# Moving steps between slots in a pooled-attention and maxout kernel: an earlier first sum, a shorter warm-up, batches 1 and 2 re-slotted, a split last store

## The chip, the cores and the metric

One core of one Trainium2 chip. The metric is the device time of one execution in microseconds (us), median over executions. The span is the part of it that the trace covers, from the first to the last instruction; it is shorter than the time by 1.8 us on average in nearly all kernels here. All runs compared are in the fast state, unless a single run's state is unknown, which is said.

## The reference, cut to what matters

```python
# q, k, v: (8 batches, 8 heads, 576 rows, 64); w1, w2, w3: (512, 768); w_out: (768, 512)
k_p = k.reshape(B, H, 72, 8, D).mean(axis=3)          # pool 8 rows of k and of v
v_p = v.reshape(B, H, 72, 8, D).mean(axis=3)
attn = softmax(q @ k_p.T / sqrt(D))
x = (attn @ v_p)  -> (4608 tokens, 512)
h = max(x @ w1, x @ w2, x @ w3)
out = h @ w_out                                       # (4608, 512) float32
```

## The kernel before

TensorE (PE) is fed by one hand-ordered program. The tokens go in nine blocks of 512: for each block a *hidden* stage (three products and their maximum) and a *project* stage (four output blocks of 128 tokens, `po`). The attention of the next batch is cut into steps (`pool_k`, `turn_k`, `turn_q`, `scores`, `values`, `turn_x`) that are put between the pieces of hidden and project. A piece is called a slot. The steps wait on copies by VectorE (DVE) and ScalarE (ACT), so a step in too early a slot stalls PE.

The names that matter: `turn_k` transposes the pooled k and fills `kz` with two DVE copies, `turn_q` transposes q (`pqt` to `qT`), `scores` gives `psc`, whose exponential is `et`, `values` gives `pav` and then `rcp` and `xn` on DVE ("v0" to "v4"), `turn_x` transposes `xn` (`pxt`) and copies it to `xT` ("x0" to "x4"), which the hidden stage (`pw`) reads.

```python
    heat(16)                                  # 16 warm-up matmuls, then per third of k:
    for i in (0, 2, 4):
        c = slice(i, i + 2)
        nc.vector.tensor_tensor(out=k16[:, c], in0=kts[0][:, c, 0:4],
                                in1=kts[0][:, c, 4:8], op=ALU.add)
        for p in pkp0:
            for j in range(4):
                nc.tensor.matmul(p[:, c], identh[0:96, :], k16[:, c, j, :], ...)
        if i > 0:
            ...                               # copies of the sums to kp, on DVE and ACT
        if i < 4:
            heat(1)
# ... batch 1: its steps between the slots of block 0
    steps = {19: 1, 20: 1, 21: 1, 22: 1, 23: 1, 24: 2, 25: 2, 26: 2}
    out1 = outputs(1)                         # v0 v1 x0 v2 x1 v3 x2 v4 x3 x4, xT copies on ACT
# ... batch 2: its steps between the slots of block 1
    PLAN1 = (9, 11, 13, 15, 18, 19, 20, 21, 22, 23, 24, 25, 26, 26, 27, 27, 28, 28, 29,
             29, 30, 30)
# ... the output blocks
            po = psp.tile([128, C], F32, name="po", tag="pw", bufs=3)
            ...                               # 6 matmuls of 512 columns into po
            nc.scalar.copy(out=osb, in_=po)
            for u in range(2):
                nc.sync.dma_start(out=dst[:, GS[g], :], in_=osb[64 * u:64 * u + 64, :])
```

The softmax here doesn't subtract the row's maximum and nothing guards it: scores larger than these inputs give would overflow.

Of the kernel before, what the change touches and what calls it, by code (L numbers as in the profile page):

```python
# [10 lines left out]
ALU = mybir.AluOpType  # L11
# [3 lines left out]
def kernel(  # L15
# [11 lines left out]
    nc = tc.nc  # L27
    dt = mybir.dt
    F32, BF16, F16 = dt.float32, dt.bfloat16, dt.float16

    B, H, S, D = q.shape
    POOL = 8
    Sp = S // POOL
    C = H * D
# [7 lines left out]
    NG = 9  # L42
    GS = (0, 2, 4, 6, 8, 1, 3, 5, 7)
# [157 lines left out]
    def new_et(b):  # L201
        ets[b] = sb2.tile([Sp, H, S], F16, name="et", tag="et")
# [37 lines left out]
    def queries(b):  # L240

        new_et(b)
        for m, (n0, n1) in enumerate(((0, 5), (5, 10), (10, 14), (14, 18))):
            turn_q(b, n0, n1, nc.scalar.copy, TR)
            yield
            if m == (3 if b == 2 else 2) and b > 1:
                turn_k(b)
                yield
        for h in range(H):
            scores(b, h)  # L250
            yield

    def outputs(b, tags=(TR,) * 5):

        last = None
        for (c0, keep), tag in zip(CHUNKS, tags):
            xn = values(b, c0)
            yield
            if last:
                turn_x(*last)  # L260
                yield
            last = (b, c0, keep, xn, tag)
        turn_x(*last)
        yield

# [31 lines left out]
    def project(n, hT):  # L297
        for mm in range(4):
            m = 4 * n + mm
            po = psp.tile([128, C], F32, name="po", tag="pw", bufs=3)  # L300
            for jc in range(JCH):
                nc.tensor.matmul(po, hT[:, jc, bass.ts(mm, 128)],  # L302
                                 wo_sb[:, jc, :],
                                 start=(jc == 0), stop=(jc == JCH - 1))
            osb = sb3.tile([128, C], F32, name="osb", tag="osb", bufs=5)
            nc.scalar.copy(out=osb, in_=po)  # L306
            for u in range(2):
                b, g = divmod(2 * m + u, NG)
                dst = out[S * b:S * b + S, :].rearrange("(r g) c -> r g c", g=NG)
                nc.sync.dma_start(out=dst[:, GS[g], :], in_=osb[64 * u:64 * u + 64, :])  # L310
            yield
# [7 lines left out]
    def heat(n):  # L319
        for _ in range(n):  # L320
            nc.tensor.matmul(wm, warm[:, 0:128], warm, start=True, stop=True)  # L321
# [6 lines left out]
            for _ in range(2)]  # L328
    heat(16)
    for i in (0, 2, 4):  # L330
        c = slice(i, i + 2)
        nc.vector.tensor_tensor(out=k16[:, c], in0=kts[0][:, c, 0:4],
                                in1=kts[0][:, c, 4:8], op=ALU.add)
        for p in pkp0:
            for j in range(4):
                nc.tensor.matmul(p[:, c], identh[0:96, :], k16[:, c, j, :],  # L336
                                 start=(j == 0), stop=(j == 3))
        if i > 0:
            c = slice(i - 2 if i == 2 else i, i + 2)
            nc.vector.tensor_copy(out=kps[0][:, c, 0, :], in_=pkp0[0][0:96, c])  # L340
            nc.scalar.copy(out=kps[0][:, c, 1, :], in_=pkp0[1][0:96, c])
        if i < 4:
            heat(1)
    turn_q(0, 0, 5, nc.scalar.copy, PW)
    turn_q(0, 5, 9, nc.vector.tensor_copy, ATT)
    pkt0 = [keys(0, PW) for _ in range(2)]
    for h in (0, 4):
        fill_kz(0, 0, h, h + 4, pkt0[0], nc.vector.tensor_copy)
        fill_kz(0, 1, h, h + 4, pkt0[1], nc.scalar.copy)
    heat(1)  # L350

# [14 lines left out]
    turn_q(0, 9, 14, nc.vector.tensor_copy, PW)  # L366
    turn_q(0, 14, 18, nc.scalar.copy, PW)
    pool_v(0, 0, 4, PW, nc.vector.tensor_copy)
# [13 lines left out]

    def rest():
        for c0, keep in CHUNKS[2:]:
            xn0.append(values(0, c0))
            yield
            if c0 > 256:
                turn_x(0, last, 0, xn0[-2], TR)
                yield
            last = c0  # L390
        turn_x(0, last, keep, xn0[-1], TR)
        yield


    nc.vector.memset(kz_all[1], 0.0)
    hT0 = new_hT()
    out0 = rest()

    def early():
        pool_k(1, TR)  # L400
        yield
        turn_k(1)
        yield
        yield from queries(1)

    side = early()
    steps = {19: 1, 20: 1, 21: 1, 22: 1, 23: 1, 24: 2, 25: 2, 26: 2}
    for slot, _ in enumerate(hidden(0, hT0)):
        if slot > 0:
            next(out0, None)  # L410
        for _ in range(steps.get(slot, 0)):
            next(side)
    out1 = outputs(1)
    for mm, _ in enumerate(project(0, hT0)):
        if mm == 0:
            pool_v(1, 0, 4, TR, nc.scalar.copy)
            next(side)
            pool_v(1, 4, 8, PW, nc.vector.tensor_copy)
        next(side, None)
        if mm > 0:  # L420
            next(out1)
        if mm > 1:
            next(out1)
# [8 lines left out]
    def batch(b):  # L432
        yield from queries(b)
        yield from outputs(b)


    PLAN = (2, 4, 5, 6, 8, 8, 9, 10, 11, 12, 13, 14, 15, 16, 17, 18, 18, 19, 19, 20,
            20, 21)
    PLAN1 = (9, 11, 13, 15, 18, 19, 20, 21, 22, 23, 24, 25, 26, 26, 27, 27, 28, 28, 29,
             29, 30, 30)  # L440
    for n in range(1, TOK // NB):
# [50 lines left out]
```

## Time and profile before

| | before |
|---|---|
| time, median of 3 | 264.79 us (264.77 to 265.23) |
| profiled execution | 265.15 us, span 263.4 |
| first hidden stage starts | 18.98 us |
| PE gaps in batch 1 (30 to 57 us) | 4.0 us |
| PE gaps in batch 2 (65 to 84 us) | 1.6 us |
| last output block's first matmul to the end of the span | 6.1 us |

A gap is counted from the start of the last matmul plus its steady spacing to the start of the next; the prediction below has the spacings. Warm-up matmuls count as work in this sum although they give nothing.

The table doesn't show where the clock of the array turns from half to full speed. In the timeline of the kernel before (start, duration, engine, line, operation, tiles, count, then the idle time ahead and what ended it):

```profile
6.99 0.15 PEld L321 LDWEIGHTS <-warm 128*128 128x128 bf16 x1 [0.28 <-issue]
7.33 0.10 PEld L321 LDWEIGHTS <-warm 128*128 128x128 bf16 x1 [0.20 <-issue]
...
8.86 0.42 DVE L340 CAST kp<-pkp 96x256 bf16<-96x256 f32 x1 [1.74 <-PE pkp L336]
...
18.98 1.04 PE L272 MATMUL pw<-xT,mw 128*128 128x256 f16 x8
```

The warm-up's weight loads stand 0.43 us apart up to 6.99, then 0.34, then 0.22. The step of 0.34 is part slow and part fast, so the clock turned at about 7.25 us. DVE waited 1.74 us for the sums of k before it could copy them.

### The profile page before, as it was taken

To read this page: it belongs to the slowest core of one execution; us is meant where nothing else is said; L and a number is where in the kernel's file an instruction comes from. 1 tells how busy PE (TensorE), PEld (TensorE's weight loads), DVE (VectorE), ACT (ScalarE), POOL (GpSimd) and SP (SyncE) were. 2 spreads that over 40 slices of the span, in tenths; PEclk is the share of its full clock that TensorE was granted. 3 is DMA by queue.
4 is the path that set the end of the run, shared out by engine and by line. 5 is a ranking of instruction groups with operands and counts; after the bars stand their busy time and mean duration, and the time that the engine had idled before them with its cause. 6 is when DMAs were issued, how large, how long until landed. Compare 5 with 4: busy or idle time off the path is not lost.

```text
span 263.4 us, 4734 instructions
## 1 busy us (share of the span) xinstructions
PE 251.3 (95%) x1900; PEld 142.1 (54%) x1900; DVE 129.5 (49%) x233; ACT 131.3 (50%) x234; POOL 117.6 (45%) x84
## 2 busy tenths in 40 slices
PE   7899989889999999999999999999999999999992
PEld 2678646477455555555555555555555554444441
DVE  3567552365544546364635564455446554523440
ACT  1374247546555474647464646564656553133221
POOL 8563001999899999898980796000000000000000
PEclk9999999999999999999999999999999999999999
DMA  7999999887767977968987605100420042015006
GB/s 179 202 196 207 201 230 231 216 228 146 157 170 163 251 188 146 252 212 165 205 212 206 94 2 122 40 2 0 105 58 0 2 100 59 2 36 124 0 9 154
DMA packets 20867, 34.73 MB, mean 132 GB/s; under 512 B 2636, under 2 KB 13260, under 8 KB 20268
## 3 DMA queue, kind: packets, MB, share of 16 engines
q0 software_dynamic: 14048, 21.44, 41.7%
q1 hardware_dynamic: 6796, 12.98, 19.9%
q8 instruction: 15, 0.25, 0.4%
q14 instruction: 8, 0.07, 0.1%
HBM read 34.60 MB, written 9.44 MB: 167 GB/s over the span
## 4 chain that ended last, share of the span: by engine, by line
PE 89%; ACT 6%; DVE 3%; issue 1%; ACTq 0%
PE pw L272 49%; PE po L302 18%; PE psc L194 6%; PE pav L223 4%; PE pqt L159 3%; PE pxt L214 3%; PE wm L321 3%; ACT xT L218 2%; ACT et L199 2%; PE pvp L148 1%; DVE kz L171 1%; ACT osb L306 1%; PE pkt L166 1%; PE pkp L185 0%; PE pkp L336 0%
## 5 line engine op out<-in xcount | busy, mean ns | idle before, releaser
L272 PE MATMUL pw<-xT,mw 128*128 128x512 f16 (+1 forms) x720 | 158.1, 358 | 0.7 <-ACT xT L218 0.7
L272 PEld LDWEIGHTS <-mw 128*128 128x128 f16 x720 | 64.3, 98 | 48.1 <-issue 0.8
L280 DVE TENSOR_TENSOR t<-t,pw 128x512 f16<-128x512 f16 (+1 forms) x60 | 38.0, 634 | 75.3 <-PE pw L272 48.4
L302 PE MATMUL po<-mwo,hT 128*128 128x512 f16 x216 | 51.5, 379 | 0.0
L277 ACT CAST t<-pw 128x512 f16<-128x512 f32 (+1 forms) x60 | 32.6, 543 | 37.0 <-PE pw L272 35.6
L199 ACT ACTIVATE et<-psc 72x576 f16<-72x576 f32 (+2 forms) x62 | 40.6, 662 | 12.2 <-PE psc L194 12.2
L283 DVE TENSOR_TENSOR hT<-t,pw 128x512 f16<-128x512 f16 (+1 forms) x60 | 38.0, 633 | 12.3 <-PE pw L272 9.2
L127 POOL TENSOR_TENSOR vt<-vt 72x2048 f32<-72x2048 f32 (+1 forms) x12 | 41.2, 3431 | 3.1 <-DMA vt<-in_v_dram 2.6
L127 POOL TENSOR_TENSOR kt<-kt 96x1536 f32<-96x1536 f32 (+1 forms) x12 | 31.5, 2623 | 22.8 <-DMA kt<-in_k_dram 22.2
L306 ACT COPY osb<-po 128x512 f32<-128x512 f32 x36 | 21.1, 585 | 40.4 <-PE po L302 40.4
L161 ACT COPY qT<-pqt 128x640 bf16<-128x640 bf16 (+1 forms) x30 | 19.2, 639 | 23.9 <-PE pqt L159 23.9
L302 PEld LDWEIGHTS <-hT 128*128 128x128 f16 x216 | 19.3, 97 | 19.7 <-DVE hT L283 1.7
L231 DVE TENSOR_TENSOR xn<-pav,rcp 128x512 f16<-128x512 f32 x40 | 27.7, 691 | 1.4
L194 PE MATMUL psc<-qT,kz 128*128 128x64 bf16 (+3 forms) x192 | 26.2, 246 | 0.8 <-DVE kz L171 0.5
L194 PEld LDWEIGHTS <-kz 128*128 128x128 bf16 x192 | 17.8, 98 | 15.2 <-DVE kz L171 1.6
L218 ACT COPY xT<-pxt 128x512 f16<-128x512 f16 (+1 forms) x39 | 21.3, 546 | 3.2 <-PE pxt L214 3.1
L223 PE MATMUL pav<-vp,et 72*128 72x65 f16 x320 | 17.6, 194 | 1.7 <-ACT et L199 1.7
L223 PEld LDWEIGHTS <-et 72*128 72x128 f16 x320 | 15.3, 98 | 6.1 <-ACT et L199 1.5
L229 DVE RECIPROCAL rcp<-pav 128x8 f32<-128x8 f32 x40 | 8.2, 205 | 18.2 <-PE pav L223 18.2
L214 PE MATMUL pxt<-identh,xn 128*128 128x128 f16 x160 | 15.5, 219 | 1.0 <-ACT xT L218 0.5
L214 PEld LDWEIGHTS <-xn 128*128 128x128 f16 x160 | 11.5, 97 | 9.0 <-DVE xn L231 2.4
L159 PEld LDWEIGHTS <-qb 128*128 128x128 bf16 x144 | 10.0, 97 | 8.3 <-issue 2.7
(42 smaller groups left out, 113.4 us busy)
## 6 DMA issues: line engine op xcount, KB each, us to landing
out_dram<-osb SPq DMA_DIRECT2D x72, 128.0 KB, 2.4
kt<-in_k_dram POOLq DMA_DIRECT2D x5, 1152.0 KB, 7.8
vt<-in_v_dram POOLq DMA_DIRECT2D x5, 1152.0 KB, 9.8
qb<-in_q_dram POOLq DMA_DIRECT2D x7, 576.0 KB, 13.4
mw<-in_moe_w_dram POOLq DMA_DIRECT2D x9, 256.0 KB, 9.9
kt<-in_k_dram SPq DMA_DIRECT2D x3, 384.0 KB, 5.2
kt<-in_k_dram SPq DMA_DIRECT2D x1, 1152.0 KB, 9.6
vt<-in_v_dram SPq DMA_DIRECT2D x1, 1152.0 KB
```

What stands on the lines that cost most here:

```text
L127: e.tensor_tensor(out=t[:, :, 0:n, :], in0=t[:, :, 0:n, :], in1=t[:, :, n:2 * n, :], op=ALU.add)
L194: nc.tensor.matmul(out, kz_all[b % 2][:, f % 2, h, :], qTs[b][:, n + i0:n + i1, 64 * (h % 2):64 * (h % 2) + 64], start=True, stop=True)
L199: nc.scalar.activation(out=out, in_=in_, func=FT.Exp, scale=1.0 / 64.0)
L214: nc.tensor.transpose(pxt[:, kc, :], xn[:, kc // 2, 2 * (kc % 2):2 * (kc % 2) + 2, :], identh)
L218: evac(out=xT[:, :, g0 + keep:g0 + 128], in_=pxt[:, :, keep:128])
L223: nc.tensor.matmul(pav[:, h // 4, 65 * (h % 4):65 * (h % 4) + 65], ets[b][:, h, c0:c0 + 128], vp_all[:, b, h, :], start=True, stop=True)
L231: nc.vector.tensor_tensor(out=xn, in0=pv[:, :, :, 0:D], in1=rcp.to_broadcast([128, 2, 4, D]), op=ALU.mult)
L272: nc.tensor.matmul(pw, w_sb[wi][:, kc, bass.ts(jc, 128)], xT[:, kc, col], start=(kc == 0), stop=(kc == KCH - 1))
L277: nc.scalar.copy(out=t, in_=pw)
L280: nc.vector.tensor_tensor(out=t1, in0=t, in1=pw, op=ALU.max)
L283: nc.vector.tensor_tensor(out=hT[:, jc, c0:c1], in0=t, in1=pw, op=ALU.max)
L302: nc.tensor.matmul(po, hT[:, jc, bass.ts(mm, 128)], wo_sb[:, jc, :], start=(jc == 0), stop=(jc == JCH - 1))
```

## The change

Its intent is to close the gaps: start the first sum of k before 16 warm-up matmuls are over, move the steps of batches 1 and 2 so that fewer of them wait, put the xT copies of batch 1 on DVE, and let the end of the last store travel earlier. The core of the diff:

```diff
@@ steps of a batch: the order becomes a string, the copy engine an argument
-            if m == (3 if b == 2 else 2) and b > 1:
+            if m == (3 if b == 2 else 2):
                 turn_k(b)
-    def outputs(b, tags=(TR,) * 5):
+    def outputs(b, order="v0 v1 x0 v2 x1 v3 x2 v4 x3 x4", tag=TR, evac=nc.scalar.copy):
@@ project(): the last tile in two column halves
+            last = m == TOK // 128 - 1
+            for c in ((slice(0, C // 2), slice(C // 2, C)) if last else (slice(0, C),)):
 [...]
+                if c.start:
+                    nc.vector.tensor_copy(out=osb[:, c], in_=po)
+                else:
+                    nc.scalar.copy(out=osb[:, c], in_=po)
+                    (nc.scalar if last and u else nc.sync).dma_start(
+                        out=dst[:, GS[g], c], in_=osb[64 * u:64 * u + 64, c])
@@ start
-    heat(16)
-    for i in (0, 2, 4):
 [...]
+    heat(10)
+    add_k0(0)
+    sum_k0(0)
+    heat(3)
+    add_k0(2)
+    sum_k0(2)
+    heat(2)
+    put_k0(0, 4)
+    add_k0(4)
+    sum_k0(4)
+    put_k0(4, 6)
 [... q copies of batch 0 change engine, a later heat(1) goes ...]
@@ batch 1
-        yield from queries(1)
+        for m, (n0, n1) in enumerate(((0, 5), (5, 10), (10, 14), (14, 18))):
+            turn_q(1, n0, n1, nc.vector.tensor_copy, TR)
+            if m > 1:
+                scores(1, m - 2)
+            yield
+        for h in range(2, H, 2):
+            scores(1, h)
+            scores(1, h + 1)
+            yield
-    steps = {19: 1, 20: 1, 21: 1, 22: 1, 23: 1, 24: 2, 25: 2, 26: 2}
+    steps = {18: 1, 19: 1, 21: 1, 22: 1, 23: 1, 24: 1, 25: 1, 26: 1}
+        if slot > 24:
+            h = 4 * (slot - 25)
+            pool_v(1, h, h + 4, TR, nc.scalar.copy)
-    out1 = outputs(1)
+    out1 = outputs(1, "v0 v1 x0 x1 v2 v3 x2 v4 x3 x4", evac=nc.vector.tensor_copy)
@@ batch 2
-        yield from outputs(b)
+        yield from outputs(b, *(("v0 v1 x0 v2 x1 x2 v3 x3 v4 x4",) if b == 2 else ()))
-    PLAN1 = (9, 11, 13, 15, 18, 19, 20, 21, 22, 23, 24, 25, 26, 26, 27, 27, 28, 28, 29,
-             29, 30, 30)
+    PLAN1 = (9, 11, 13, 15, 19, 20, 21, 22, 23, 24, 25, 26, 26, 27, 28, 28, 29, 29, 30,
+             30)
```

More of the change, by code (lines that the diff above doesn't have):

```diff
@@ L251, in queries @@
             yield
-    def outputs(b, tags=(TR,) * 5):
-        last = None
-        for (c0, keep), tag in zip(CHUNKS, tags):
-            xn = values(b, c0)
-            yield
-            if last:
-                turn_x(*last)
-                yield
-            last = (b, c0, keep, xn, tag)
-        turn_x(*last)
-        yield
+    def outputs(b, order="v0 v1 x0 v2 x1 v3 x2 v4 x3 x4", tag=TR, evac=nc.scalar.copy):
+        xns = {}
+        for step in order.split():
+            i = int(step[1])
+            c0, keep = CHUNKS[i]
+            if step[0] == "v":
+                xns[i] = values(b, c0)
+            else:
+                turn_x(b, c0, keep, xns[i], tag, evac)
+            yield
     def hidden_part(n, jc, c0, c1, hT):
@@ L299, in project @@
             m = 4 * n + mm
-            po = psp.tile([128, C], F32, name="po", tag="pw", bufs=3)
-            for jc in range(JCH):
-                nc.tensor.matmul(po, hT[:, jc, bass.ts(mm, 128)],
-                                 wo_sb[:, jc, :],
-                                 start=(jc == 0), stop=(jc == JCH - 1))
-            osb = sb3.tile([128, C], F32, name="osb", tag="osb", bufs=5)
-            nc.scalar.copy(out=osb, in_=po)
-            for u in range(2):
-                b, g = divmod(2 * m + u, NG)
-                dst = out[S * b:S * b + S, :].rearrange("(r g) c -> r g c", g=NG)
-                nc.sync.dma_start(out=dst[:, GS[g], :], in_=osb[64 * u:64 * u + 64, :])
+            last = m == TOK // 128 - 1
+            osb = sb3.tile([128, C], F32, name="osb", tag="osb", bufs=5)
+            for c in ((slice(0, C // 2), slice(C // 2, C)) if last else (slice(0, C),)):
+                po = psp.tile([128, c.stop - c.start], F32, name="po", tag="pw", bufs=3)
+                for jc in range(JCH):
+                    nc.tensor.matmul(po, hT[:, jc, bass.ts(mm, 128)], wo_sb[:, jc, c],
+                                     start=(jc == 0), stop=(jc == JCH - 1))
+                if c.start:
+                    nc.vector.tensor_copy(out=osb[:, c], in_=po)
+                else:
+                    nc.scalar.copy(out=osb[:, c], in_=po)
+                for u in range(2):
+                    b, g = divmod(2 * m + u, NG)
+                    dst = out[S * b:S * b + S, :].rearrange("(r g) c -> r g c", g=NG)
+                    (nc.scalar if last and u else nc.sync).dma_start(
+                        out=dst[:, GS[g], c], in_=osb[64 * u:64 * u + 64, c])
             yield
@@ L328, with add_k0, sum_k0, put_k0 @@
             for _ in range(2)]
-    heat(16)
-    for i in (0, 2, 4):
-        c = slice(i, i + 2)
-        nc.vector.tensor_tensor(out=k16[:, c], in0=kts[0][:, c, 0:4],
-                                in1=kts[0][:, c, 4:8], op=ALU.add)
+    heat(10)
+    def add_k0(i):
+        nc.vector.tensor_tensor(out=k16[:, i:i + 2], in0=kts[0][:, i:i + 2, 0:4],
+                                in1=kts[0][:, i:i + 2, 4:8], op=ALU.add)
+    def sum_k0(i):
         for p in pkp0:
             for j in range(4):
-                nc.tensor.matmul(p[:, c], identh[0:96, :], k16[:, c, j, :],
+                nc.tensor.matmul(p[:, i:i + 2], identh[0:96, :], k16[:, i:i + 2, j, :],
                                  start=(j == 0), stop=(j == 3))
-        if i > 0:
-            c = slice(i - 2 if i == 2 else i, i + 2)
-            nc.vector.tensor_copy(out=kps[0][:, c, 0, :], in_=pkp0[0][0:96, c])
-            nc.scalar.copy(out=kps[0][:, c, 1, :], in_=pkp0[1][0:96, c])
-        if i < 4:
-            heat(1)
-    turn_q(0, 0, 5, nc.scalar.copy, PW)
-    turn_q(0, 5, 9, nc.vector.tensor_copy, ATT)
+    def put_k0(i, j):
+        nc.vector.tensor_copy(out=kps[0][:, i:j, 0, :], in_=pkp0[0][0:96, i:j])
+        nc.scalar.copy(out=kps[0][:, i:j, 1, :], in_=pkp0[1][0:96, i:j])
+    add_k0(0)
[8 more added lines that the diff above has]
+    put_k0(4, 6)
+    turn_q(0, 0, 5, nc.vector.tensor_copy, PW)
+    turn_q(0, 5, 9, nc.scalar.copy, ATT)
     pkt0 = [keys(0, PW) for _ in range(2)]
@@ L349 @@
         fill_kz(0, 1, h, h + 4, pkt0[1], nc.scalar.copy)
-    heat(1)
     def scores4(h):
@@ L366 @@
     turn_q(0, 9, 14, nc.vector.tensor_copy, PW)
-    turn_q(0, 14, 18, nc.scalar.copy, PW)
+    turn_q(0, 14, 18, nc.vector.tensor_copy, PW)
     pool_v(0, 0, 4, PW, nc.vector.tensor_copy)
@@ L381 @@
     scores2(6)
-    def rest():
-        for c0, keep in CHUNKS[2:]:
-            xn0.append(values(0, c0))
-            yield
-            if c0 > 256:
-                turn_x(0, last, 0, xn0[-2], TR)
-                yield
-            last = c0
-        turn_x(0, last, keep, xn0[-1], TR)
-        yield
     nc.vector.memset(kz_all[1], 0.0)
     hT0 = new_hT()
-    out0 = rest()
+    out0 = outputs(0, "v2 v3 x2 v4 x3 x4")
     def early():
-        pool_k(1, TR)
+        pool_k(1, PW)
         yield
@@ L403, in early @@
         yield
-        yield from queries(1)
+        new_et(1)
+        for m, (n0, n1) in enumerate(((0, 5), (5, 10), (10, 14), (14, 18))):
[7 more added lines that the diff above has]
+            yield
     side = early()
-    steps = {19: 1, 20: 1, 21: 1, 22: 1, 23: 1, 24: 2, 25: 2, 26: 2}
+    steps = {18: 1, 19: 1, 21: 1, 22: 1, 23: 1, 24: 1, 25: 1, 26: 1}
     for slot, _ in enumerate(hidden(0, hT0)):
@@ L412 @@
             next(side)
-    out1 = outputs(1)
+        if slot > 24:
+            h = 4 * (slot - 25)
+            pool_v(1, h, h + 4, TR, nc.scalar.copy)
+    out1 = outputs(1, "v0 v1 x0 x1 v2 v3 x2 v4 x3 x4", evac=nc.vector.tensor_copy)
     for mm, _ in enumerate(project(0, hT0)):
-        if mm == 0:
-            pool_v(1, 0, 4, TR, nc.scalar.copy)
+        for _ in range((1, 0, 0, 0)[mm]):
             next(side)
-            pool_v(1, 4, 8, PW, nc.vector.tensor_copy)
-        next(side, None)
-        if mm > 0:
-            next(out1)
-        if mm > 1:
+        for _ in range((0, 1, 2, 2)[mm]):
             next(out1)
```

## The prediction

> **What bounds the kernel now.** I read the engine shares and the 40 slices first, then the chain of work that ended last, then the waits of TensorE (PE), and last the timeline around each of these waits.
>
> ```profile
> PE 251.3 (95%) x1900; PEld 142.1 (54%) x1900; DVE 129.5 (49%) x233; ACT 131.3 (50%) x234; POOL 117.6 (45%) x84
> ...
> PE   7899989889999999999999999999999999999992
> ...
> PE 89%; ACT 6%; DVE 3%; issue 1%; ACTq 0%
> ```
>
> PE is busy 95% of 263.4 us and carries 89% of the chain. VectorE (DVE) and ScalarE (ACT) are half idle, so a faster copy is worth something only where PE waits for it. PE misses about 12 us: 1.5 before its first instruction, 4.6 after its last, and 6 in gaps that all lie before 85 us, bar 0.24 us per later batch. The waits of PE in the first 80 us name them (columns: total, times, longest):
>
> ```profile
> PE pav L223 <- ACT et L199: 1.7, 3, 0.7
> PE pqt L159 <- DVE kz L171: 0.8, 1, 0.8
> PE pw L272 <- ACT xT L218: 0.7, 1, 0.7
> PE pkp L336 <- DVE k L332: 0.7, 1, 0.7
> PE pxt L214 <- ACT xT L218: 0.5, 2, 0.3
> PE psc L194 <- DVE kz L171: 0.5, 1, 0.5
> ```
>
> These idle times count from a matmul's modelled end, which includes its drain. Counted from where the stream could have gone on (start of the last matmul plus the steady spacing, 0.216 us for 512 columns, 0.109 for 256), a gap is some 0.17 us longer. So counted, batch 1 (30 to 57 us) has gaps of 0.46, 1.01, 0.34, 0.91, 0.84, 0.45, together 4.0; batch 2 (65 to 84 us) has 0.15, 0.65, 0.68, 0.11, together 1.6. One gap from the timeline shows how the others are read (start, duration, engine):
>
> ```profile
> 52.03 0.59 ACT L306 COPY osb<-po 128x512 f32<-128x512 f32 x1 [0.71 <-PE po L302]
> 52.52 0.59 ACT L218 COPY xT<-pxt 128x512 f16<-128x512 f16 x1
> 53.16 0.60 PE L272 MATMUL pw<-xT,mw 128*128 128x256 f16 x4 [0.67 <-ACT xT L218]
> ```
>
> The xT copy stands behind the output copy on ACT, and the next stage cannot start before it ends: 0.84 us lost.
>
> **What the Trainium skill says.** "TensorE: Matmul & The Clock Gate", Part 1: a cold array needs N/1.2 ns per matmul, a warm one N/2.4 + 2.5, and warming takes a busy window of about 3.4 us on a free-running clock. The trace agrees: the warm-up's weight loads stand 0.43 us apart until about 7.1 us, and 512 columns cost 0.216 later. The same page (architectural detail): PE runs matmuls in program order, ACT and DVE are strict FIFO. The trace agrees: the DVE maximum of the matmuls that ended at 65.8 us starts only at 66.70, behind two copies. "DMA: Bandwidth & Descriptors", "Issuing engines are not separate DMA queues": stores from two engines share the same 16 DMA engines and save issue time only. The trace shows them nearly full at the end (below).
>
> **Part by part.** *Start.* The first k sum has its added data at 5.57 us (DVE 4.88 + 0.69), but PE runs 16 warm-up matmuls until about 7.8. With 10, PE is free at 1.46 + 10 x 0.427 = 5.73, sums cold (8 x 0.107) to 6.6, three warm-ups to 7.5 (the clock turns at 7.1 again), second sum to 8.0 (its add is done at 7.12), so the kp copy starts at 8.0 against 8.86. Add, sum and copies follow as before; the first scores end at 11.3 against 12.36, a gain of 1.0. DVE's order of adds and copies is unchanged in the built program: what moves is PE. Then v must have landed:
>
> ```profile
> vt<-in_v_dram POOLq DMA_DIRECT2D x1, 288.0 KB, 8.4
> ...
> 12.86 1.04 PE L148 MATMUL pvp<-vt,identh 72*128 72x256 f16 x8
> ```
>
> Issued at 3.88, it lands at 12.3; PE would want it at 11.8. So 0.5 of the 1.0 becomes a wait on DMA. The last q transposes going to DVE spare the second half of the scores their wait (0.15 us at 14.1). Following exp, values and xT copies, the first hidden stage starts **0.7 us** earlier (18.3, not 18.98). The later loads have slack: k of batch 1 lands at 16.75 + 11.9 = 28.65, wanted at 29.1.
>
> *Batch 1.* pool_k moves one slot up, turn_k stays one slot (0.86 us) behind it, so its wait for both kp copies stays 0.45. But then two slots, not one, lie before the q transposes, while the two kz copies take 2 x 0.77: 1.01 becomes 0.08. q copies on DVE take 0.49, not 0.69, but stand behind the maxima: a new wait of 0.2. Scores come two at a time with their exps spread by the two pool_v: 0.34 and 0.91 vanish. The xT copy that gates the next stage now runs on DVE (0.42) instead of behind the output copy: 0.84 becomes 0.40. But in that stage's first five slots (0.44 us each) DVE must now do, besides four maxima (0.34 to 0.42), two rcp and xn pairs (0.85 each) and the x2 and x3 copies. In order, from the stage's start at t: xn3 ends at t + 1.84, maximum to 2.18, x2's copy to 2.52, maximum to 2.86, then v4's rcp and xn to 3.71, and only then x3's copy, to 4.05 (its transpose was done at 2.8). x4's transpose needs the single "tr" buffer that this copy empties, so it starts at t + 4.10, while PE has finished slot 4 at t + 3.23: 0.45 becomes 0.87. Sum: 4.0 becomes 0.45 + 0.08 + 0.2 + 0.40 + 0.87 = 2.0, a gain of **2.0**.
>
> *Batch 2.* turn_k moves from behind slot 18 (its result goes to ACT) to behind slot 19 (its maximum, 0.69, goes to DVE, ahead of the kz copies), still one slot before the scores: 0.15 + 0.65 becomes 0.58 + 0.64. v0 moves behind an output block of 1.30: 0.68 vanishes. x2, which the next stage reads, moves from behind the third to behind the fourth block: osb copy then xT copy on ACT against 0.49 us of PE work, so the 0.84 seen above comes back here. v4 now has one slot to x4, but rcp and xn wait behind a maximum: 0.66 in place of 0.11. And x4 now stands straight before the first q transposes of batch 3, in the one "tr" buffer: drain, copy, signal (0.2 + 0.37 + 0.05) give 0.62. Sum: 1.6 becomes 3.34, a loss of **1.75**.
>
> *Steady batches* (26.8 us each) keep their order: 0.
>
> *Tail.* Two halves of 12 matmuls with 256 columns take 12 x 0.109 = 1.31, as before. The last copy is 0.42 instead of 0.58, and the first half is copied 0.8 us earlier. But:
>
> ```profile
> 259.00:260.00 1.00, 0.00 (x0) 0.00 (x0) 0.00 (x0) 0.38 (x1) 0.00 (x0) 1.00 0.87 199
> 260.00:261.00 1.00, 0.00 (x0) 0.00 (x0) 0.00 (x0) 0.00 (x0) 0.00 (x0) 1.00 0.91 203
> 261.00:262.00 1.00, 0.00 (x0) 0.00 (x0) 0.00 (x0) 0.00 (x0) 0.00 (x0) 1.00 0.70 162
> ```
>
> The last two numbers of a line are the DMA share and GB/s. Blocks of 256 KB come every 1.30 us and take 1.28 at 203 GB/s, so the queue is full to 261.9 and earlier data only queues. Rows of 1 KB instead of 2 KB have more packets (in the trace's packet records, loads of 1024 B have a median of 0.098 us a packet, stores of 2048 B 0.146): up to 0.2 longer. I take **0 +- 0.3**.
>
> Sum: -0.7 - 2.0 + 1.75 + 0 = -0.95, so 263.8. My list strings waits together without letting one absorb another, which errs long; I say **263.6**.
>
> **Rivals.** (a) *All gaps close*, as the change intends: 1.0 + 4.0 + 1.6 = 6.6 and 258.2, over 2%. For it: DVE and ACT are half idle on average. Against: DVE in batch 1's handover is not, and the x2 and turn_k orders plainly add waits. (b) *Batch 2's reorder costs nothing*, the other parts as I have them: 262.1. For it: it is the part with the most steps guessed by hand. Against: the same osb-then-xT pattern shows its 0.84 at 53 us. (c) *The array stays cold*: fewer warm-ups miss the window and the first 10 us run at half rate, the start gains nothing: 264.5, or worse by a window. Against: PE stays busy without a break from 1.46 to 8.4 all the same. (d) *The tail is latency, not rate*: two queues give another 0.5 to 0.8: 263.0.
>
> **Range and chances.** (b) with (d) reaches 261.5; (c) with my batch 2 reaches 264.8 or a little over. Range 262.2 to 264.8. A 2% gain needs 259.5, nearly all of (a): 0.03. A 2% loss, 270.1, needs 5 us of new waits: 0.01.
>
> **What would show it.** Right: the first kp copy near 8.0; pvp waiting on DMA near 12.3; first pw near 18.3; no pqt wait behind kz in batch 1, but a pxt wait there of 0.7 or more; in batch 2 a pw wait on ACT xT of some 0.7 at the start of the third hidden stage, and a pqt wait on the xT copy just after. Wrong: no waits of PE between 63 and 88 us; kz waits below 0.5; warm-up spacing of 0.43 past 8 us; DMA share under 0.7 in the last 2 us of data.

## The result, and the profile after

| | before | after |
|---|---|---|
| time, median | 265.01 us of 4 runs, one of them new (264.77 to 265.35) | 264.37 us of 4 runs (264.15 to 264.55) |
| ratio | | 0.9974, interval 0.9957 to 0.9992 |

A ratio here is the mean time of one kernel's fast runs over the mean of the other's of the same rounds, so it is not quite the ratio of the medians quoted. The change is worth 0.64 us by the medians. The time lies inside the predicted range, but the forecast gain, 264.79 - 263.6 = 1.2 us, is twice what was measured.

The page of the changed kernel, in the same three views as before (engine shares, slices, shares of the chain that ended last):

```profile
PE 250.3 (95%) x1902; PEld 142.6 (54%) x1902; DVE 132.7 (51%) x243; ACT 125.9 (48%) x225; POOL 117.6 (45%) x84
...
PE   7899999988997999999999999999999999999992
...
PE 87%; DVE 4%; ACT 4%; issue 1%; DMA 1%; SPq 0%; DVEq 0%
```

PE is the bound as it was; work went from ACT to DVE (ACT 131.3 to 125.9 us, DVE 129.5 to 132.7). A slice is 6.6 us: the dips of the sixth and eighth (33 to 39 and 46 to 53 us) are filled, and the tenth and the thirteenth (59 to 66 and 79 to 85 us) have new ones. The waits of PE up to 90 us in the trace after name them (columns: total, times, longest):

```profile
...
PE psc L194 <- DVE kz L171: 1.2, 3, 0.5
PE pxt L214 <- DVE xT L218: 0.7, 1, 0.7
PE pw L272 <- ACT xT L218: 0.7, 1, 0.7
PE pxt L214 <- DVE xn L231: 0.6, 1, 0.6
PE pqt L159 <- ACT xT L218: 0.5, 1, 0.5
PE pkp L343 <- DVE k L337: 0.5, 1, 0.5
PE pav L223 <- ACT et L199: 0.4, 1, 0.4
PE pkt L166 <- ACT kp L188: 0.3, 1, 0.3
...
```

The q transposes of batch 1 no longer wait long enough for `kz` to be listed. Of the waits on `et` (1.7 us before) one of 0.4 is left, at 15.4 us in the start; those of batches 1 and 2 are gone. The wait of `pxt` on the xT copy by DVE is new and is batch 1's. Two of the three `kz` waits, `pw` on ACT's xT, `pxt` on `xn` and `pqt` on the xT copy lie in batch 2. The timeline says where. First the start of the kernel after:

```profile
7.97 0.42 DVE L347 CAST kp<-pkp 96x256 bf16<-96x256 f32 x1 [1.20 <-PE pkp L343]
...
vt<-in_v_dram POOLq DMA_DIRECT2D x1, 288.0 KB, 7.9
...
11.98 1.04 PE L148 MATMUL pvp<-vt,identh 72*128 72x256 f16 x8
...
17.95 1.04 PE L272 MATMUL pw<-xT,mw 128*128 128x256 f16 x8
```

(The `vt` line is from the DMA view, the rest from the timeline.) The copy starts 0.89 us sooner than in the trace before, the pooling of v 0.88 and the first hidden stage 1.03. The first part of v, issued at 3.88 in both traces, landed at 11.76 here and at 12.27 before. So v was there when PE came for it at 11.98, and the wait on DMA that the prediction named as a sign is absent. Then the handover of batch 1 to its hidden stage:

```profile
52.70 0.69 DVE L231 TENSOR_TENSOR xn<-pav,rcp 128x512 f16<-128x512 f32 x1
53.30 0.41 DVE L218 COPY xT<-pxt 128x512 f16<-128x512 f16 x1
...
53.77 0.38 PE L214 MATMUL pxt<-identh,xn 128*128 128x128 f16 x4 [0.68 <-DVE xT L218]
```

The copy of x3 stands behind the `xn` of v4 on DVE, and the next transpose needs the buffer that this copy empties: the predicted wait. And batch 2:

```profile
64.21 0.31 PE L194 MATMUL psc<-qT,kz 128*128 128x320 bf16 x1 [0.39 <-DVE kz L171]
...
78.65 0.58 ACT L310 COPY osb<-po 128x512 f32<-128x512 f32 x1 [0.71 <-PE po L305]
79.13 0.59 ACT L218 COPY xT<-pxt 128x512 f16<-128x512 f16 x1
79.77 1.02 PE L272 MATMUL pw<-xT,mw 128*128 128x512 f16 x4 [0.68 <-ACT xT L218]
...
84.44 0.44 PE L159 MATMUL pqt<-ident,qb 128*128 128x128 bf16 x5 [0.46 <-ACT xT L218]
```

The output copy ahead of the xT copy on ACT, then `pw` waiting: it is the pattern that batch 1 had before at 53 us, now in batch 2. With gaps counted as in the prediction:

| stage | gaps before | gaps predicted | gaps after |
|---|---|---|---|
| batch 1 | 0.46, 1.01, 0.34, 0.91, 0.84, 0.45 = 4.0 | 0.45, 0.08, 0.2, 0.40, 0.87 = 2.0 | 0.46, 0.15, 0.27, 0.42, 0.85 = 2.15 |
| batch 2 | 0.15, 0.65, 0.68, 0.11 = 1.6 | 0.58, 0.64, 0.84, 0.66, 0.62 = 3.34 | 0.56, 0.65, 0.84, 0.74, 0.63 = 3.42 |

Last, the end of the kernel after, in 1 us windows (after the clock stand the DMA share and GB/s):

```profile
259.00:260.00 1.00, 0.00 (x0) 0.00 (x0) 0.00 (x0) 0.00 (x0) 0.00 (x0) 0.91 0.87 250
260.00:261.00 1.00, 0.00 (x0) 0.00 (x0) 0.00 (x0) 0.00 (x0) 0.00 (x0) 0.50 0.59 172
261.00:262.00 1.00, 0.00 (x0) 0.00 (x0) 0.00 (x0) 0.00 (x0) 0.00 (x0) 0.50 0.00 0
```

The span ends at 262.3 here and at 263.4 before. From the first matmul of the last output block to the end of the span it is 6.18 us after and 6.09 before (from the start of the last matmul, 4.98 and 5.01).

So in the two batches the traces agree with the forecast nearly gap by gap, and their spans differ by 1.1 us, close to the forecast. That the sum agrees is partly luck: the start gained 1.03 for a forecast of 0.7, with v landing 0.5 us sooner in the trace after, and the two batches together gained 0.03 for a forecast of 0.25. Yet over all runs the kernels differ by about half of that. The question for the experiments is which part the time does not pay.

### The profile page after: what moved, and what is told of

It reads as the page before. It is cut to its first block, busy times and chain, and to the rows that moved or that the text cites. A ratio compares the mean times of both kernels' runs of the same rounds, so it can differ in the third digit from the quotient of the medians.

```text
span 262.3 us, 4747 instructions
## 1 busy us (share of the span) xinstructions
PE 250.3 (95%) x1902; PEld 142.6 (54%) x1902; DVE 132.7 (51%) x243; ACT 125.9 (48%) x225; POOL 117.6 (45%) x84
## 4 chain that ended last, share of the span: by engine, by line
PE 87%; DVE 4%; ACT 4%; issue 1%; DMA 1%; SPq 0%; DVEq 0%
PE pw L272 49%; PE po L305 16%; PE psc L194 6%; PE pav L223 4%; PE pqt L159 3%; PE pxt L214 3%; PE wm L326 2%; ACT xT L218 2%; PE pvp L148 1%; DVE t L280 1%; DMA out_dram<-osb 1%; ACT et L199 1%; DVE xn L231 1%; PE pkt L166 1%; DVE kz L171 1%
## 5 line engine op out<-in xcount | busy, mean ns | idle before, releaser
L305 PE MATMUL po<-mwo,hT 128*128 128x512 f16 (+1 forms) x222 | 51.5, 373 | 0.0
L310 ACT COPY osb<-po 128x512 f32<-128x512 f32 (+1 forms) x36 | 20.8, 579 | 38.7 <-PE po L305 38.5
L305 PEld LDWEIGHTS <-hT 128*128 128x128 f16 x222 | 19.9, 97 | 19.4 <-DVE hT L283 1.7
L194 PE MATMUL psc<-qT,kz 128*128 128x64 bf16 (+3 forms) x192 | 25.6, 246 | 1.2 <-DVE kz L171 1.2
L161 ACT COPY qT<-pqt 128x512 bf16<-128x512 bf16 (+1 forms) x25 | 15.9, 637 | 21.5 <-PE pqt L159 21.5
L218 ACT COPY xT<-pxt 128x512 f16<-128x512 f16 (+1 forms) x34 | 18.6, 547 | 4.3 <-PE pxt L214 4.2
L229 DVE RECIPROCAL rcp<-pav 128x8 f32<-128x8 f32 x40 | 8.2, 204 | 18.4 <-PE pav L223 18.3
```

The costliest lines, as they stand in the source:

```text
L194: nc.tensor.matmul(out, kz_all[b % 2][:, f % 2, h, :], qTs[b][:, n + i0:n + i1, 64 * (h % 2):64 * (h % 2) + 64], start=True, stop=True)
L218: evac(out=xT[:, :, g0 + keep:g0 + 128], in_=pxt[:, :, keep:128])
L305: nc.tensor.matmul(po, hT[:, jc, bass.ts(mm, 128)], wo_sb[:, jc, c], start=(jc == 0), stop=(jc == JCH - 1))
```

## The experiments

Sixteen runs were made, three of them repeats of a kernel unaltered, all with correct results. They came in five calls on four different chips; each call had its own runs of the kernel before, and kernels of different calls are compared through their ratios to it. "Mean" below is the mean over fast runs. Of the spans the means are quoted too, since a part of the time lies outside the span.

### The change again, and its parts alone

`again` is the changed kernel unaltered.

> The changed kernel once more, for a tighter interval and a second trace. My theory: the gaps of PE add up, so the gain is what the two traces show, 1.1 us (ratio 0.9958); where single runs differ, the loads of v in the first 12 us landed later and the first pooling of v waits for them (up to 0.5 us). Rival: the two profiled runs were a lucky pair and the true gain is that of the medians, 0.6 to 0.7 us (0.9975), with the difference spread over the whole span.

Measured: 264.16 us median against 264.63, ratio 0.9986 (0.997 to 1.0002); mean time 0.37 lower, mean span 0.34 lower. The first result was 0.64. Both say that the gain is a few tenths, well under 1.2.

`after_oldb2` is the changed kernel with the slots and the order of batch 2 as before:

```diff
-        yield from outputs(b, *(("v0 v1 x0 v2 x1 x2 v3 x3 v4 x4",) if b == 2 else ()))
+        yield from outputs(b)
-    PLAN1 = (9, 11, 13, 15, 19, 20, 21, 22, 23, 24, 25, 26, 26, 27, 28, 28, 29, 29, 30, 30)
+    PLAN1 = (9, 11, 13, 15, 18, 19, 20, 21, 22, 23, 24, 25, 26, 26, 27, 27, 28, 28, 29, 29, 30, 30)
```

> The changed kernel with the steps of batch 2 where they were before. My theory: the move of batch 2 costs 1.7 to 1.8 us, so this is faster than the changed kernel by that: ratio to before about 0.989 (2.9 us less), and the gaps of PE at the start of the third hidden stage (0.84), before x4 (0.74) and before the first q transposes of batch 3 (0.63) are gone. Rival (the move costs nothing, its waits only take up slack that returns elsewhere): same time as the changed kernel, ratio 0.996 to 0.9975.

Measured: 262.24 us, ratio 0.9915 (0.9901 to 0.9929). Against `again` in the same rounds the mean is 1.89 us lower. The waits of PE between 57 and 90 us in its trace are back to two:

```profile
PE pav L223 <- ACT et L199: 0.5, 1, 0.5
PE psc L194 <- DVE kz L171: 0.5, 1, 0.5
```

So the reorder of batch 2 costs 1.9 us, against 1.75 predicted; rival (b), that it costs nothing, is out. Without it the change would have been worth over 2 us.

`b1_only` is the kernel before with only the parts of batch 1 (the block marked "batch 1" in the diff above, with the step order that it needs).

> The kernel before with the moves of batch 1 alone. My theory: 4.0 us of gaps become 2.1, so 1.9 to 2.0 us faster than before, ratio 0.9925; the one new gap, 0.85 before x4, stays. Rival (the gaps of batch 1 only closed because the start came earlier and the loads had landed): under 1.2 us, ratio above 0.9955.

Measured: 262.87 us, ratio 0.9931 (0.9914 to 0.9949); mean time 1.83 lower, mean span 1.79 lower. From the start of the first hidden stage to the end its trace takes 242.43 us, against 244.40 in the trace before: 1.97, which is the predicted 2.0. Batch 1 pays, alone and with the rest.

`start_only` is the kernel before with only the new start.

> The kernel before with the new start alone. My theory: 1.0 us faster where v lands by 11.9 us, 0.6 where it lands at 12.3, on the mean 0.8: ratio 0.997. Rival (the gain of the start is lost again on the way, in a later wait for a load): under 0.3 us, ratio above 0.999.

Measured: 264.52 us, ratio 1.0003 (0.9983 to 1.0022). Mean span 0.41 lower, but the time did not fall: in this kernel 2.29 us lie outside the span on average, from 1.77 to 2.96, against 1.82 in the runs of before beside it. The trace shows one thing that goes with it. In the DMA view of 262 to 265 us, after the last instruction, stands a packet of the instruction queue (kind, packets, MB, share):

```profile
q8 instruction: 1, 0.02, 2.0%
```

It has 16 KB and runs from 263.8 to 264.8 us, in a span that ends at 262.06. Of the 18 traces here only this one and that of `heat10` below (262.6 to 263.7, span 262.09) have it so late; in the other sixteen the last packet of that queue starts 8 to 10 us before the end. These two are also the kernels with the fewest instructions (4727 and 4722, 4734 or more in the others), and the only ones with more time outside the span. So a late instruction fetch is the likely reason; no run isolates it. The changed kernel has no such packet, so there the start's gain in span can reach the time. The start's worth was measured once more from the other side.

`nostart` is the changed kernel with the old start (the block marked "start" put back).

> The changed kernel with the start of the kernel before. My theory: how late the old start is depends on when the array's clock turns, which differs from run to run (6.7 and 7.1 us in two traces of it), and the new start runs into the loads of v and of k of batch 1, so the new start is worth 0.3 to 0.5 us on the mean, not 0.7 to 1.0: this kernel has a mean span of about 262.9 against 262.45 for the changed kernel, ratio to before about 1.0005. Rival (the start is worth the 1.0 us seen between the first two traces): mean span 263.4, slower than before, ratio 1.0025.

Measured: 264.46 us, ratio 1.000 (0.9985 to 1.0015), mean span 262.68 against 262.69. Against `again` (0.9986; other rounds, so only through the ratios) that leaves about 0.37 us for the start, with intervals that overlap. A sharper pair: `nostart` against `k1early` below, the changed kernel with one load moved, differs by 0.50 us in mean time (0.2 either way, from the spread of the runs) and 0.47 in mean span, some of it the load's. These measures, with 0.41 (span, alone; 0.3 either way) and, below, 0.41 (traces), lie near 0.4; 0.7 is at the edge of the sharper ones.

`tail_only` is the kernel before with only the split last tile.

> The kernel before with the last tile stored in column halves on two queues. My theory: the DMA engines are full in the last 5 us, so the time from the last matmul to the end stays within 0.15 us of before, ratio 1.000. Rival (the tail is latency, halves and a second queue shorten it): 0.4 to 0.8 us less, ratio 0.9975.

Measured: 264.35 us, ratio 0.9997 (0.9981 to 1.0013); mean time 0.07 lower. The tail is worth nothing measurable, as predicted; rival (d), 0.5 to 0.8 us, is out.

### Why the start is worth 0.4 and not 0.7

Two theories were open. One: the new start runs into the landing of v and gives back part of its gain. The other: the trace before, on which the 0.7 rests, was a late one, since the clock turns at another time in each run, and the old start follows the clock while the new one does not.

`before_a` and `before_b` are the kernel before, unaltered, each for one more trace.

> The kernel before, one more trace. My theory: the time of the first hidden stage goes with the time at which the spacing of the warm-up matmuls falls from 0.43 to 0.22 us, as in the four traces of the old start so far (5.5: 18.05, 6.7: 18.67, 7.1: 18.88, 7.2: 18.98), so a turn near t gives 18.05 + 0.55 x (t - 5.5), to 0.2 us. Rival: no such relation.

> The kernel before once more, for one more point of the same relation: a turn near t gives a first hidden stage at 18.05 + 0.55 x (t - 5.5), to 0.2 us.

Measured: 264.56 and 264.08 us (single runs, state unknown). The trace of `before_b`:

```profile
4.85 1.43 PEld L321 LDWEIGHTS <-warm 128*128 128x128 bf16 x7 [0.27 <-issue]
...
7.70 0.42 DVE L340 CAST kp<-pkp 96x256 bf16<-96x256 f32 x1 [0.92 <-PE pkp L336]
...
11.80 1.05 PE L148 MATMUL pvp<-vt,identh 72*128 72x256 f16 x8
...
17.82 1.03 PE L272 MATMUL pw<-xT,mw 128*128 128x256 f16 x8
```

It is the kernel of the prediction's profile, but from 4.85 us seven weight loads fit in 1.43 us, so the clock had turned by 4.9 instead of 7.25. The kp copy starts at 7.70 instead of 8.86, *earlier than in the trace of the changed kernel* (7.97), and the first hidden stage at 17.82 instead of 18.98. After that they hardly differ: from the start of the first hidden stage to the end, the three traces of before take 244.40, 244.40 and 244.38 us. All of the difference of their spans, 263.38, 262.79 and 262.20, is the start's.

The relation (18.05 us and 0.55 more for each us of a later turn, to 0.2 us) held in `before_b`, 17.73 expected and 17.82 measured, and missed in `before_a`, 17.97 expected and 18.39 measured. There v landed late, so the clock's turn alone does not set the start.

All traces with the old start and 16 warm-ups, by the moment of the clock's turn (us):

| kernel | clock turns | first part of v landed | pooling of v starts | first hidden stage |
|---|---|---|---|---|
| before | 7.25 | 12.27 | 12.86 | 18.98 |
| tail_only | 7.04 | 12.27 | 12.76 | 18.88 |
| b1_only | 6.63 | 11.83 | 12.55 | 18.67 |
| before_a | 5.36 | 12.36 | 12.41 | 18.39 |
| nostart | 5.31 | 11.90 | 11.94 | 18.05 |
| before_b | 4.92 | 11.76 | 11.80 | 17.82 |

With a late turn PE comes to the pooling of v 0.5 to 0.7 us after v has landed; with an early one it starts 0.05 us after the landing in all three, and v decides. (The profile puts the wait in `before_a` down to a q copy on DVE; in `nostart` and `before_b` that copy ended 0.4 us after the pooling had started, so it does not hold it up.) The new start has no first kind: in eight traces that keep the new start and the order after it (after, again, after_oldb2, start_only, turnk18, k1early, xact, best) the pooling starts 0.13 to 0.22 us after v landed, whenever the clock turned (from 4.4 us in start_only to 7.25 in after). Their first hidden stages start at 17.67 to 18.60, mean 18.05; the six of the old start have a mean of 18.47. The difference is 0.41 us, of which 0.14 can be chance, since v landed at 11.92 on average in these eight and at 12.06 in the six. Counted from v's landing, the first hidden stage comes after 6.13 us on average with the new start, after 6.61 to 6.84 with the old one and a late turn, and after 6.03 to 6.15 with the old one and an early turn. Both theories hold, then: v's landing bounds the new start, and the new start takes away the dependence on the clock, which at the same landing is worth 0.5 to 0.7 us in a run where the clock turns late and about nothing where it turns early. The 1.03 us of the first pair of traces is such a late turn and 0.5 us of v's earlier landing.

`heat10` is the kernel before with `heat(10)` for `heat(16)` and nothing else.

> The kernel before with 10 warm-up matmuls in place of 16 and nothing else. My theory: the old start is late only because the 16 warm-ups run cold until the clock turns (between 5.5 and 7.2 us), so the shorter warm-up alone brings the gain of the start: first kp copy near 8.0 us whatever the turn, first hidden stage at 17.7 to 18.2 us, mean span 0.3 to 0.4 us under before, ratio about 0.9987. Rival (the gain comes from the other evacuation engines): first hidden stage as late as before for the same turn (18.7 to 19.0 at 6.7 to 7.2), ratio 1.000.

Measured: 264.33 us, ratio 0.9995 (0.9975 to 1.0016); mean span 0.33 lower (0.5 either way), 2.05 us outside the span. Its trace (clock turned at 5.17) has the kp copy at 7.22, sooner than the 8.0 expected, and the first hidden stage at 17.69. With so early a turn the old start is not late either (17.82 in `before_b`), so this trace does not test a late turn. That the shorter warm-up alone brings the gain of the start is likely by the span, but not shown; by the time neither it nor `start_only` is told from nothing.

### What of batch 2 costs, and what a better order gives

`turnk18` is the changed kernel with `turn_k` of batch 2 one slot earlier.

```diff
-    PLAN1 = (9, 11, 13, 15, 19, 20, 21, ...
+    PLAN1 = (9, 11, 13, 15, 18, 20, 21, ...
```

> The changed kernel with the k transposes of batch 2 back behind slot 18 and its scores left at slot 20. My theory: the gaps of 0.56 and 0.65 us before the first scores close to 0.1, so 1.1 us less than the changed kernel, ratio to before 0.9945; the gaps of 0.84, 0.74 and 0.62 after it stay. Rival (the score wait only takes time that would be waited later): no change, 0.9985.

Measured: 263.17 us, ratio 0.995 (0.9935 to 0.9965): 1.0 us below `again` by the ratios. Its waits of PE between 57 and 90 us:

```profile
PE pw L272 <- ACT xT L218: 0.7, 1, 0.7
PE pxt L214 <- DVE xn L231: 0.6, 1, 0.6
PE pqt L159 <- ACT xT L218: 0.5, 1, 0.5
```

The `kz` wait is gone and the other three stand: gaps add up, and closing 1.2 us of them (0.56 + 0.65) gave 1.0 us of time by the ratios.

`k1early` is the changed kernel with the load of batch 1's k ahead of the last third of the weights, since `again` had shown a wait of 0.2 us on it.

> The changed kernel with the load of batch 1's k ahead of the last third of the weights. My theory: the pooling of that k, which waits 0.2 to 0.3 us for the load in some traces of the new start, no longer waits: 0.1 to 0.3 us less than the changed kernel on the mean, and the rest of the gain of the start comes through. Rival: the wait for k hid another one (the weights moved back now come late), same or slower.

Measured: 264.03 us, ratio 0.998 (0.9964 to 0.9997). Its trace has no wait on that load. The gain over `again`, 0.0006 of the time or 0.16 us, is within the noise.

`xact` is `after_oldb2` with the xT copies of x2 to x4 of batch 1 on ACT.

```diff
-                turn_x(b, c0, keep, xns[i], tag, evac)
+                turn_x(b, c0, keep, xns[i], tag, evac if i < 2 else nc.scalar.copy)
```

> The changed kernel with batch 2 as before, and with the copies of x2, x3 and x4 of batch 1 back on ScalarE (x0 and x1 stay on VectorE). My theory: the gap of 0.85 us before x4 is VectorE's queue, so it shrinks to 0.45 as before the change: 0.4 us less than the same kernel without this edit (ratio to before 0.9915), so about 0.990. Rival (the gap is the one-buffer transpose slot whatever engine empties it): stays at 0.85, ratio 0.9915.

```profile
53.99 0.38 PE L214 MATMUL pxt<-identh,xn 128*128 128x128 f16 x4 [0.29 <-ACT xT L218]
```

The wait of x4 fell as expected (its gap from 0.85 to 0.45), and from the first hidden stage to the end the trace takes 242.15 us instead of 242.69. The time did not fall: 262.57 us, ratio 0.9924 (0.9904 to 0.9944), against 0.9915. In this trace v landed at 12.42 instead of 11.58 and the first hidden stage started at 18.60 instead of 17.69. One trace of each cannot tell whether that is the kernel's doing, the run's or the chip's (`xact` and `best` ran on another chip than `after_oldb2`).

`best` joins what had helped: `after_oldb2`, the load of `k1early`, the copies of `xact`, x2 and x4 of batch 1 one slot later, `turn_k` and one later step of batch 2 one slot earlier.

```diff
-    out1 = outputs(1, "v0 v1 x0 x1 v2 v3 x2 v4 x3 x4", evac=nc.vector.tensor_copy)
+    out1 = outputs(1, "v0 v1 x0 x1 v2 v3 -- x2 v4 x3 -- x4", evac=nc.vector.tensor_copy)
-    PLAN1 = (9, 11, 13, 15, 18, 19, 20, 21, 22, 23, 24, 25, 26, 26, 27, ...
+    PLAN1 = (9, 11, 13, 15, 17, 19, 20, 21, 22, 23, 24, 25, 25, 26, 27, ...
```

> The new start and tail, batch 1 with x2 to x4 copied by ScalarE, v3 moved ahead of the second hidden stage and a free slot before x4, batch 2 in the old order with its k transposes one slot earlier (17) and two scores at slot 25, k of batch 1 loaded before the last third of the weights. My theory, gap by gap: batch 1 from 4.0 us to about 1.1 (0.46 and some 0.15, 0.27, 0.13, 0.1 stay), batch 2 from 1.6 to 0.3, start 0.4: 4.6 us less than before, ratio 0.9825, span mean 258.1. Rival (waits that close here open elsewhere, since VectorE and ScalarE have the same work in less time): under 3 us, ratio above 0.989.

Measured: 260.60 us over 4 runs, ratio 0.9857 (0.9834 to 0.988): 3.8 us below the kernel before, for 4.6 expected, and the fastest here by its median. From the first hidden stage to the end its trace takes 240.28 us, 2.41 less than `after_oldb2`, which is about the sum of the gaps closed (3.7 to 1.3). But its first hidden stage started 0.8 us later, and its trace has a wait that was shorter in `turnk18` and `k1early` (0.36 and 0.39, with v landed at 11.9; 12.4 here):

```profile
PE pvp L149 <- DMA vt<-in_v_dram: 0.7, 1, 0.7
```

`vlate` (the changed kernel), `best2` and `vlate2` (`best`) try to fill that wait. The first two put the second half of the scores ahead of the first pooling of v; `vlate2` puts a third group of scores there as well.

```diff
-    pool_v(0, 0, 4, PW, nc.vector.tensor_copy)
     scores4(4)
+    pool_v(0, 0, 4, PW, nc.vector.tensor_copy)
```

> The changed kernel with the second group of batch 0's scores ahead of the first pooling of v, whose load lands at 11.6 to 12.4 us. My theory: what the new start has left to wait for is that load, so with the scores in the wait the first hidden stage starts 0.5 to 0.8 us earlier in the trace (near 17.3 us) and the time falls by 0.4 to 0.7 against the changed kernel: ratio to before about 0.996 (0.9986 without). Part of it may stop at the load of batch 1's k (28.6 to 29.1 us). Rival (the copies and exps behind it set the pace, not the load): no change.

> The best version so far with the same exchange. There the first pooling of v waited 0.88 us in the trace and k of batch 1 is loaded early. My theory: 0.6 to 0.9 us less than that version's 0.9857: ratio about 0.983, span mean 258.3. Rival: no change, 0.9857.

> The best version with both the second group of scores and the first pair of the next group ahead of all three poolings of v. The last exchange gained nothing because the three poolings then stood ahead of those scores and held up the exps. My theory: with them gone from that place the exps follow each other and the first hidden stage starts 0.4 to 0.8 us earlier than in the best version's trace (18.48): near 17.8, ratio about 0.983. Rival (the load of v is not what the start waits for at all): 0.9857.

Measured: `vlate` 264.36 us, 0.9986 (`again` had 0.9986); `best2` 260.77, 0.9854; `vlate2` 260.91, 0.9862 (`best` had 0.9857). No exchange gained anything. In the trace of `vlate` the scores moved ahead wait for q copies on DVE instead, and the first hidden stage starts at 18.34. The theory that the wait on v can be filled with scores fell in this form. That v's landing alone is the floor of the start isn't supported either: in `vlate2` v landed at 11.66 and the first hidden stage still started at 18.74. What would start it sooner stays open.

## Why the prediction was right or wrong

By its own sum (us; the measured worth is the difference of mean times, for the start that of the ratios of `again` and `nostart`):

| step | predicted | measured | by |
|---|---|---|---|
| start | -0.7 | -0.4 | nostart against again; span of start_only (its time: +0.06); first hidden stage over 14 traces |
| batch 1 | -2.0 | -1.8 | b1_only |
| batch 2 | +1.75 | +1.9 | after_oldb2 against again |
| tail | 0 | -0.07 | tail_only |
| sum | -0.95 | -0.37 | the measured terms, and `again` itself |

**The step that failed** is the start, "the first hidden stage starts **0.7 us** earlier (18.3, not 18.98)". The mechanism was right: with the clock turning at 7.25 in both profiled runs, the kp copy came at 7.97 for a forecast of 8.0, and PE reached the pooling of v at 11.98 for 11.8; where v landed at 12.4 (`xact`, `best`) the hidden stage came at 18.5 to 18.6, near the 18.3. The size was off, because 18.98 is no property of the kernel. It is one run of it, with the latest clock turn of the six traces of the old start. Over these six, the old start reaches the hidden stage at 18.47 on average, the new one at 18.05.

The forecast even erred against the new start, which is 0.25 better than 18.3 since v landed at 11.6 to 12.4 and not always at 12.3, but the baseline was 0.5 too late. So the trap was to subtract from one traced run: at a late turn and the same landing of v the new start is worth 0.5 to 0.7, near the forecast; over the runs it is not. The prediction had said that the clock's window runs free; it took the turn of one run as a constant all the same ("the clock turns at 7.1 again"; by the spacing it was 7.25). A smaller miss in the same step is "later loads have slack": k of batch 1 landed at 28.4 to 29.2 us in the traces with the load in its old place, and in `again` and `after_oldb2` its pooling started 0.3 us late, just after the landing.

**The last step failed as well**, the shading from 263.8 to 263.6 because the "list strings waits together without letting one absorb another, which errs long". No run supports it. In the traces the gaps of batch 2 add up to 3.42 for 3.34, `turnk18` took away two and left the other three, and in `best` 2.4 us of closed gaps are 2.4 us of the trace. In time, `b1_only` paid 1.8 us of the trace's 1.97 and `turnk18` 1.0 of 1.2; `best` is 1.5 below `after_oldb2` by the ratios, and its start, 0.8 later in the trace, accounts for the rest of the 2.4.

**Batch 1** was right in mechanism and, nearly, in size: the `kz` wait of the q transposes 0.15 for 0.08, the exps' waits gone, the new wait of x4 0.85 for 0.87. The time paid 1.8 of the trace's 1.97. **Batch 2** was right in each of its five gaps within 0.1 us, and the 1.9 us of `after_oldb2` against `again` shows that it gives back nearly all that batch 1 gains. **The tail** was right in its worth. Its reason, full DMA engines, is not shown: in the trace after, the share in the last window with data is 0.59, which the prediction had named as a sign against it, and the rate reached 250 GB/s where 203 was taken for full. The last packet ended 4.78 us after the first matmul of the last block, 4.63 before; what holds it there was not isolated. Over all traces the span ends 6.08 to 6.11 us after that matmul with the tile whole and 5.91 to 6.68 with it split, 6.2 on average, so the split gains nothing in the span either.

**The rivals**: (a), all gaps close, is out by the gaps of batch 2; (b) and (d) are out by `after_oldb2` and `tail_only`; (c), the array stays cold, by the trace of the changed kernel, whose clock turned at the same 7.25.

Two things stay open. The kernels with the old batches and a changed start, `start_only` and `heat10`, have 0.2 to 0.5 us more outside the span than all others, so their gain in span did not reach the time; the late instruction packet in both traces goes with it, but was not isolated. And the first result (0.64) and `again` (0.37) differ by 0.3, which is inside their intervals.

## What to carry to other kernels

Before sizing a change of the first microseconds, take several traces of the kernel before: here one and the same program reached its first real stage at 17.82, 18.39 and 18.98 us, a spread larger than the gain that was forecast from one of them. Here the gaps of the engine that bounds the kernel added up and could be summed by hand to a tenth of a microsecond, for the losses of a reorder as well as for its gains. When a change of several parts moves the time little, test the parts alone first: here one part gained 1.8 us and another lost 1.9, and the gaps that are left in the trace name the better order, which ran 3.8 us below the kernel before.

## What the Trainium skill lacked or had wrong

- "TensorE: Matmul & The Clock Gate", Part 1: it gives the transition a run-to-run spread of plus or minus 500 ns, and says elsewhere in the same part that the count of cold matmuls varies with the run. Here the clock turned between 4.4 and 7.25 us, 3.0 to 5.8 us after the first warm-up matmul at 1.46, a spread of 2.8 us. Its advice not to fit to a specific cold count is what the prediction should have followed; what it lacks is that a start which waits on its warm-up hands this spread to the time (first hidden stage 17.82 to 18.98 us), and that the new start, with 10 warm-ups first, did not in eight traces: its pooling of v followed the landing by 0.13 to 0.22 us.
- "DMA: Bandwidth & Descriptors", "Issuing engines are not separate DMA queues": nothing here contradicts it. Column halves and a second issuing engine for the last tile, together, were worth 0.07 us in `tail_only`, which is within the noise. The second engine alone was not tested.
- No page that the prediction drew on says how far the landing of one and the same load moves from run to run: the first part of v landed at 11.57 to 12.42 us in the traces here, with the same loads ahead of it.
- No page says that a program's last instruction fetch can run after its last instruction. In `start_only` and `heat10`, where the traces show it so late, 2.29 and 2.05 us lie outside the span on average, and 1.8 in the others; that the one causes the other was not isolated.
